# The first batch's biases added on GpSimd in SBUF, instead of by products with a row of ones

## The chip, the cores and the metric

One core of one Trainium2 chip runs the whole program. The metric is the device time of one launch in microseconds (us), median of several runs; less is better. TensorE does the matrix products (PE in the profile, its weight loads PEld), VectorE is DVE, ScalarE is ACT, GpSimd is POOL, and SyncE (SP) issues all of this kernel's DMAs, in order.

## The reference

For each of 8 batches of 3008 rows with 256 columns: a real Fourier transform along the rows, a complex linear layer on each frequency, a soft threshold at 0.01, the inverse transform, and then a feed-forward block on all 24064 rows.

```
X  = rfft(x, axis=1)
Yr = Xr @ w_r - Xi @ w_i + b_r
Yi = Xr @ w_i + Xi @ w_r + b_i
Y  = sign(Y) * max(|Y| - 0.01, 0)        # real and imaginary part apart
x2 = irfft(Y).reshape(24064, 256)
h  = x2 @ w_in                           # 256 -> 2048
out = (h - tanh(h)) @ w_out              # 2048 -> 256
```

## The kernel before

**Three products for the complex layer.** With the sum s = Xr + Xi there is one common product t1 = s @ w_r, and the two parts are Yr = t1 + Xi @ w3 + b_r and Yi = t1 + Xr @ w2 + b_i, where w3 = -(w_r + w_i) and w2 = w_i - w_r. The two products that belong to one part each stand side by side in one PSUM bank, `vv` (512 columns), and t1 has a bank of its own (256 columns, tag `o0`, a single buffer).

**Stages.** At the start the first batch's rows are transformed over one factor of the length (L291) and written to DRAM (`a`). Then comes the stage of the change: twelve units (`WholeSpectrum`, L516), which share out the frequencies of the first batch, go through the second transform (`dft`, L534), the linear layer (`cross`, L544; the last unit `cross_apart`, L559), the threshold and the first step of the inverse (`inverse`, L605), and write to DRAM (`z`). After the stage the second inverse step (L667) makes the first two chunks of rows, and the feed-forward block starts (`up`, L703, and `down`, L733). All later batches go through the same mathematics in pieces laid between the products of the feed-forward block, by other functions (`Spectrum`, L376); their biases were added by VectorE from a tile `bias` already (L447).

**The loop over units (L854 to L900), and the order of the work.** Each engine runs its instructions in the order in which the program emits them. One pass of the loop is called turn i here. Turn i emits, among others:

- `common` of unit i-2: ScalarE copies t1 out of PSUM into `tb`
- `dft` of unit i: TensorE's products, and ScalarE's copy `xf`
- on ScalarE, from turn 3 on, steps of a weight conversion (`ends` is two activations, `parts` a cast with a subtraction on GpSimd, L250)
- `shrink` of unit i-2: VectorE's `blend` adds tb and vv (L579), then ScalarE's `above` and `below` (L586, L590)
- `sum` of unit i on VectorE (L542), which `cross` of unit i needs one turn later
- `cross` of unit i-1 on TensorE; its t1 reuses the one bank, so it waits for the ScalarE copy of the unit before
- in even turns the inverse of units i-4 and i-3, with four ScalarE copies `zo`
- in turns 2, 3 and 4 one split of a linear weight in two parts (`split_lin`, L818): a ScalarE cast, and a subtraction, in turns 2 and 4 on GpSimd and in turn 3 on VectorE
- on VectorE the rest of the weight conversion (L221 to L245), and `join` of unit i-2 (L603), which the inverse needs

In the last turn `sum` comes ahead of `shrink`. After the loop units 10 and 11 are finished in a row of their own (L901 to L919).

**The weight conversion.** The feed-forward weights come as 64-bit floats and are turned into pairs of 32-bit words block by block, by the steps named above; the blocks' raw words (`w_raw`) are loaded by SP, the first at the end of turn 0.

**The biases before.** 33 partitions of SBUF get the two biases in one row (L165, called from L160). `combine_linear` (L168) makes from them a tile `brow` in which row 0 holds the rounded bias, row 32 what the rounding left, and all others zero, and a tile `ones`. In `cross` one product of `ones` with `brow` (L551; L567 twice in `cross_apart`) writes the biases into vv before the other products add to it.

**SP's order around the stage.** SP issues the stores of `a` (L309, L313) and the first units' loads (`at`, L388); the last four L313 stores are followed by turn 0's load of the first `w_raw` (L195), and then by turn 1's load `at` of unit 4, which needs those stores landed.

Of the kernel before, what the change touches and what calls it, by code (L numbers as in the profile page):

```python
# [92 lines left out]


@with_exitstack
def spectral_ffn(ctx, tc, x, w_r, w_i, w_in, w_out, x_fold, b_turned, f1, f1b, f1f, f2, f2f, i1, i1w, i2, out):
    nc = tc.nc
    P = 128
    w_in, w_out = w_in.bitcast(U32), w_out.bitcast(U32)
# [55 lines left out]
    def load_linear():  # L155
        wr = ffn.tile([P, 2, D], F32, name="wr_f", tag="g_h")
        wi = ffn.tile([P, 2, D], F32, name="wi_f", tag="g_l")
        nc.sync.dma_start(out=wr, in_=w_r.rearrange("(t p) e -> p t e", p=P))
        nc.sync.dma_start(out=wi, in_=w_i.rearrange("(t p) e -> p t e", p=P))
        rows = load_bias(work.tile([33, 2, D], F32, name="bias_rows", tag="tmp", bufs=4), 33)  # L160
        return wr, wi, rows

    def load_bias(dst, n):
        both = b_turned.rearrange("(o k) d -> o (k d)", o=1).to_broadcast([n, 2 * D])
        nc.sync.dma_start(out=dst.rearrange("p k d -> p (k d)"), in_=both)  # L165
        return dst

    def combine_linear(wr, wi, rows, zero):  # L168
        w2 = ffn.tile([P, 2, D], F32, name="w2_f", tag="g_h")
        w3 = ffn.tile([P, 2, D], F32, name="w3_f", tag="g_h")  # L170
        nc.vector.scalar_tensor_tensor(out=w3, in0=wr, scalar=-1.0, in1=wi, op0=ALU.mult, op1=ALU.subtract)
        nc.gpsimd.tensor_tensor(out=w2, in0=wi, in1=wr, op=ALU.subtract)
        ones = work.tile([P, P], F32R, name="ones", tag="s_l")
        nc.vector.tensor_scalar(out=ones, in0=zero[:, :P], scalar1=1.0, scalar2=None, op0=ALU.add)
        top = work.tile([33, 2 * D], F32R, name="bias_top", tag="tmp", bufs=4)
        flat = rows.rearrange("o r e -> o (r e)")
        nc.scalar.copy(out=top, in_=flat)
        brow = work.tile([P, 2 * D], F32R, name="brow", tag="ot", bufs=1)
        nc.vector.tensor_copy(out=brow, in_=zero)
        nc.vector.tensor_copy(out=brow[0:1], in_=top[0:1].bitcast(F32))  # L180
        nc.vector.tensor_tensor(out=brow[32:33], in0=flat[32:33], in1=top[32:33].bitcast(F32), op=ALU.subtract)
        return (wr, w2, w3), (ones, brow)

    win_h = const.tile([P, 2, FF], F32R, name="win_h")
    win_l = const.tile([P, 2, FF], F32R, name="win_l")
# [330 lines left out]
    class WholeSpectrum(Spectrum):  # L516
# [27 lines left out]
        def cross(self):  # L544
            if self.jp % 3 < 2:
                self.vv = ps_h.tile([P, 512], F32, name="ps_v", tag="h")
            else:
                self.vv = ps_o.tile([P, 512], F32, name="ps_v", tag="o1")
            ones, brow = bias_rows
            by_part = self.vv.rearrange("p (r i j) -> p r i j", r=2, j=2)  # L550
            nc.tensor.matmul(by_part, ones, brow.rearrange("p (r j i) -> p r i j", r=2, j=2), start=True, stop=False)  # L551
            self.t1 = ps_o.tile([P, 512], F32, name="ps_t1", tag="o0")[:, :D]
            for k, (dst, lhs) in enumerate((
                (self.vv[:, :D], self.xf[:, :, 1]), (self.vv[:, D:], self.xf[:, :, 0]), (self.t1, self.sf),
            )):
                for t in range(2):
                    nc.tensor.matmul(dst, lhs[:, t], whole_lin[2 - k][:, t, :], start=k == 2 and t == 0, stop=k > 0 and t == 1)

        def cross_apart(self):  # L559
            ones, brow = bias_rows  # L560
# [4 lines left out]
            for dst, lhs, w, b in ((self.t1, self.sf, 0, None), (low, self.xf[:, :, 1], 2, 0), (high, self.xf[:, :, 0], 1, D)):  # L565
                if b is not None:
                    nc.tensor.matmul(paired(dst, D), ones, in_turn(brow[:, b:b + D]), start=True, stop=False)  # L567
                for t in range(2):
                    nc.tensor.matmul(dst, lhs[:, t], whole_lin[w][:, t, :], start=b is None and t == 0, stop=t == 1)

        def common(self):
            self.tb = work.tile([P, D], F32, name="tb0", tag="xi")
            nc.scalar.copy(out=self.tb, in_=self.t1)

        def blend(self):
            self.y = self.temp("y", "g")
            if not hasattr(self, "sides"):
                both = self.vv.rearrange("p (r d) -> p r d", r=2)
                nc.vector.tensor_tensor(out=self.y, in0=self.tb.unsqueeze(1).to_broadcast([P, 2, D]), in1=both, op=ALU.add)  # L579
                return  # L580
            for r, side in enumerate(self.sides):
                nc.vector.tensor_tensor(out=self.y[:, r], in0=self.tb, in1=side, op=ALU.add)

        def above(self):
            self.up = self.temp("up", "th")
# [180 lines left out]
    with tc.manual_schedule(engines={E.PE, E.Activation, E.DVE, E.Pool, E.SP}):  # L766
# [18 lines left out]
        lin_in = load_linear()  # L785
# [68 lines left out]
        for i in range(NU):  # L854
            if i + 2 == NU:
                for c in range(2):
                    waves[c].tile()
                    waves[c].load_part(0, LATE - 8)
            if i + 1 == NU:
                for c in range(2):  # L860
                    waves[c].load_part(LATE - 8, LATE)
            if unit(i - 2):
                unit(i - 2).common()
            unit(i).dft()
            if i + 1 == NU:
                unit(i).sum()
            for op in on_act.get(i, ()):
                op()
            if unit(i - 2):
                unit(i - 2).shrink()  # L870
            if i + 1 < NU:
                unit(i).sum()
            if unit(i - 1):
                unit(i - 1).cross()
            if 0 < i < NU - 3:
                units[i + 3].load()
            if i in turns:
                load_turns(*units[turns[i]:turns[i] + 2])
            if i == NU - 3:
                for u in units[-4:]:  # L880
                    u.load_turn()
            if i > 2 and i % 2 == 0:
                pair = units[i - 4:i - 2]
                pair[1].inverse(banks=pair[0].inverse(), first=D)
                for u in pair:
                    u.put()
            if i < len(early):
                early[i].load()
            if i == 4:
# [94 lines left out]
        for g in range(-2, FIXED):  # L984
            c, f = steps[g + 2]
            ready[g + 2] = chunks[c].up(f, plan.get(g, ()))
            if g == -2:
                forward(6)
                forward(7)
                blocks[1].load()  # L990
                load_bias(bias, P)
# [163 lines left out]
```

## Time and profile before

| | us |
|---|---|
| median of three runs (2443.18 to 2443.49) | 2443.32 |
| the profiled execution | 2442.45 |
| its span, first to last instruction | 2440.7 |

| engine | busy us | share of the span | instructions |
|---|---|---|---|
| PE | 2429.0 | 100% | 19274 |
| DVE | 1779.9 | 73% | 3251 |
| ACT | 1348.6 | 55% | 2781 |
| POOL | 34.5 | 1% | 31 |

The shares are means over the whole program. The stage of the change lies between 25.7 and 85 us, so it has to be read by stretches of its own. A timeline row gives the start of an instruction, its duration, its engine and line, and in brackets how long the engine was idle before it and what ended that. The chain of waits gives start, length and what the end of the program hung on at that time. The granted TensorE clock is a share of full speed: 1.00 is 2.4 GHz, 0.50 is 1.2 GHz.

### The profile page before, as it was taken

To read this page: it belongs to the slowest core of one execution; us is meant where nothing else is said; L and a number is where in the kernel's file an instruction comes from. 1 tells how busy PE (TensorE), PEld (TensorE's weight loads), DVE (VectorE), ACT (ScalarE), POOL (GpSimd) and SP (SyncE) were. 2 spreads that over 40 slices of the span, in tenths; PEclk is the share of its full clock that TensorE was granted. 3 is DMA by queue.
4 is the path that set the end of the run, shared out by engine and by line. 5 is a ranking of instruction groups with operands and counts; after the bars stand their busy time and mean duration, and the time that the engine had idled before them with its cause. 6 is when DMAs were issued, how large, how long until landed. Compare 5 with 4: busy or idle time off the path is not lost.

```text
span 2440.7 us, 47556 instructions
## 1 busy us (share of the span) xinstructions
PE 2429.0 (100%) x19274; PEld 2139.4 (88%) x19274; DVE 1779.9 (73%) x3251; ACT 1348.6 (55%) x2781; POOL 34.5 (1%) x31
## 2 busy tenths in 40 slices
PE   9999999999999999999999999999999999999999
PEld 6798888888888898888888889888898999888888
DVE  5887887787777776777767777677776767755555
ACT  5665555555555555555555555555555555555554
POOL 2110000000000000000000000000000000000000
PEclk9999999999999999999999999999999999999999
DMA  8533226322533212332123331322211121111000
GB/s 262 183 100 113 84 67 152 92 74 78 145 87 105 79 53 66 98 98 69 61 71 101 82 94 53 81 82 80 63 61 46 59 58 43 52 34 26 21 9 17
DMA packets 135146, 195.31 MB, mean 80 GB/s; under 512 B 13521, under 2 KB 99631, under 8 KB 134928
## 3 DMA queue, kind: packets, MB, share of 16 engines
q1 hardware_dynamic: 134928, 192.29, 27.3%
q8 instruction: 151, 2.47, 0.4%
q14 instruction: 67, 0.55, 0.1%
HBM read 114.12 MB, written 78.12 MB: 79 GB/s over the span
## 4 chain that ended last, share of the span: by engine, by line
PE 93%; DVE 4%; ACT 1%; DMA 1%; issue 0%; SPq 0%; ACTq 0%; DVEq 0%
PE o L742 39%; PE h L709 38%; PE ps_v L423 4%; PE ps_i L667 3%; PE ps_t L423 2%; PE ps_f L507 2%; PE ps_f L343 1%; DVE g L723 1%; PE ps_i L479 1%; PE ps_i L480 1%; PE ps_i L478 1%; PE ps_f L291 1%; DVE gl L729 1%; DVE w_s L242 0%; DVE w_f L239 0%
## 5 line engine op out<-in xcount | busy, mean ns | idle before, releaser
L726 ACT CAST gh<-g 128x502 fp32r<-128x502 f32 (+2 forms) x768 | 469.1, 611 | 570.7 <-DVE g L723 561.1
L729 DVE TENSOR_TENSOR gl<-g,gh 128x502 fp32r<-128x502 f32 (+2 forms) x768 | 522.1, 680 | 332.0 <-ACT gh L726 322.0
L723 DVE TENSOR_TENSOR g<-h,th 128x502 f32<-128x502 f32 (+2 forms) x768 | 520.4, 678 | 219.7 <-ACT th L720 214.5
L720 ACT ACTIVATE th<-h 128x502 f32<-128x502 f32 (+2 forms) x768 | 454.1, 591 | 379.1 <-PE h L709 374.8
L742 PE MATMUL o<-gh,wout_l 128*128 128x502 f32 (+2 forms) x1536 | 587.6, 383 | 0.2 <-DVE ot L760 0.2
L742 PE MATMUL o<-gh,wout_h 128*128 128x502 f32 (+2 forms) x1536 | 576.9, 376 | 0.0
L742 PE MATMUL o<-gl,wout_h 128*128 128x502 f32 (+2 forms) x1536 | 576.5, 375 | 0.0
L709 PE MATMUL h<-yh,win_l 128*128 128x502 f32 (+2 forms) x1536 | 452.6, 376 | 1.1 <-DVE g L723 1.0
L709 PE MATMUL h<-yh,win_h 128*128 128x502 f32 (+2 forms) x1536 | 451.0, 375 | 0.0
L709 PE MATMUL h<-yl,win_h 128*128 128x502 f32 (+2 forms) x1536 | 450.7, 375 | 0.0
L742 PEld LDWEIGHTS o<-gh,wout_l 128*128 128x128 f32 x1536 | 290.4, 189 | 53.8 <-issue 11.7
L709 PEld LDWEIGHTS h<-yh,win_l 128*128 128x128 f32 x1536 | 289.3, 189 | 39.3 <-DVE g L723 4.1
L742 PEld LDWEIGHTS o<-gl,wout_h 128*128 128x128 f32 x1536 | 290.4, 189 | 35.5 <-DVE gl L729 0.8
L709 PEld LDWEIGHTS h<-yh,win_h 128*128 128x128 f32 x1536 | 291.0, 189 | 34.3 <-issue 0.2
L709 PEld LDWEIGHTS h<-yl,win_h 128*128 128x128 f32 x1536 | 291.1, 190 | 33.9
L742 PEld LDWEIGHTS o<-gh,wout_h 128*128 128x128 f32 x1536 | 291.0, 189 | 26.4
L465 DVE TENSOR_TENSOR y<-tb,ps_v 64x256 f32<-64x256 f32 x336 | 140.0, 417 | 3.4
L700 ACT CAST yh<-yt 128x470 fp32r<-128x470 f32 (+38 forms) x200 | 89.4, 480 | 23.4 <-PE h L709 21.6
L701 DVE TENSOR_TENSOR yl<-yt,yh 128x470 fp32r<-128x470 f32 (+38 forms) x200 | 81.9, 428 | 16.0 <-ACT yh L700 15.1
L411 DVE TENSOR_TENSOR xl<-ps_f,xh 128x256 fp32r<-128x256 f32 x168 | 63.6, 419 | 27.5 <-ACT xi L409 26.0
L667 PEld LDWEIGHTS ps_i<-i,zin 48*64 48x64 f32 x4096 | 67.1, 138 | 9.5 <-issue 5.4
L667 PE MATMUL ps_i<-i,zin 48*64 48x47 f32 x4096 | 72.6, 235 | 1.6 <-DMA zin<-z 1.6
(116 smaller groups left out, 2110.3 us busy)
## 6 DMA issues: line engine op xcount, KB each, us to landing
xt<-in_x_fold SPq DMA_DIRECT2D x52, 512.0 KB
at<-a SPq DMA_DIRECT2D x96, 256.0 KB
z<-zo SPq DMA_DIRECT2D x92, 256.0 KB
zin<-z SPq DMA_DIRECT2D x92, 240.0 KB
a<-st SPq DMA_DIRECT2D x216, 96.0 KB
out<-ot SPq DMA_DIRECT2D x29, 502.0 KB
turn_l<-turns SPq DMA_DIRECT2D x72, 128.0 KB
turn_h<-turns SPq DMA_DIRECT2D x72, 128.0 KB
```

The costliest lines, as they stand in the source:

```text
L411: nc.vector.tensor_tensor(out=xl[:, s], in0=whole[s], in1=xh[:, s].bitcast(F32), op=ALU.subtract)
L423: nc.tensor.matmul(paired(dst, D), lhs[:, t], in_turn(rhs[:, t, :]), start=n == 0, stop=n == 5)
L465: nc.vector.tensor_tensor(out=self.y[ri * 64:(ri + 1) * 64, jj, :], in0=self.tb[rows, ri, :], in1=self.side(ri)[rows], op=ALU.add,)
L667: nc.tensor.matmul(pv[h][64 * c:64 * c + 64, t, 47 * k:47 * k + 47], self.zt[rows, k, at:at + 64], i2t[rows, :47], start=True, stop=True,)
L700: nc.scalar.copy(out=yh, in_=y)
L701: nc.vector.tensor_tensor(out=yl, in0=y, in1=yh.bitcast(F32), op=ALU.subtract)
L709: nc.tensor.matmul(paired(h, n), lhs[:, t, f * P:(f + 1) * P], moving(rhs[:, t], n), start=k == 0, stop=k == 5,)
L720: nc.scalar.activation(out=th[:, :n], in_=h[:, :n], func=AF.Tanh)
L723: nc.vector.tensor_tensor(out=g[:, :n], in0=h[:, :n], in1=th[:, :n], op=ALU.subtract)
L726: nc.scalar.copy(out=gh[:, :n], in_=g[:, :n])
L729: nc.vector.tensor_tensor(out=gl[:, :n], in0=g[:, :n], in1=gh[:, :n].bitcast(F32), op=ALU.subtract)
L742: nc.tensor.matmul(paired(self.o[t], n), lhs[:, f, t * P:(t + 1) * P], in_turn(rhs[:, :n]), start=f == 0 and k == 0, stop=f == NF - 1 and ...
```

## The change

The products with the row of ones go, with the tiles `brow` and `ones` and the load of 33 rows. The two biases are loaded into `bias` on all 128 partitions (256 KB) right after the last stores of `a`, ahead of the first `w_raw`. `common` still copies t1 by ScalarE, and then GpSimd adds t1's copy, taken twice, and the two biases into a tile `tb` of 512 columns; `blend` adds that to vv. For units 10 and 11 a VectorE instruction adds t1 from PSUM and the biases (`common_at_once`). `sum` comes ahead of `shrink` in every turn. Later, the load that filled `bias` for the other batches overwrites it with the biases in their other order.

```diff
@@ load_linear, load_bias, combine_linear
-        rows = load_bias(work.tile([33, 2, D], F32, name="bias_rows", tag="tmp", bufs=4), 33)
-        return wr, wi, rows
-    def load_bias(dst, n):
-        both = b_turned.rearrange("(o k) d -> o (k d)", o=1).to_broadcast([n, 2 * D])
+    def load_bias(dst, biases):
+        both = biases.rearrange("(o k) d -> o (k d)", o=1).to_broadcast([P, 2 * D])
         nc.sync.dma_start(out=dst.rearrange("p k d -> p (k d)"), in_=both)
...
-        ones = work.tile([P, P], F32R, name="ones", tag="s_l")
-        nc.vector.tensor_scalar(out=ones, in0=zero[:, :P], scalar1=1.0, scalar2=None, op0=ALU.add)
...
-        nc.scalar.copy(out=top, in_=flat)
-        brow = work.tile([P, 2 * D], F32R, name="brow", tag="ot", bufs=1)
-        nc.vector.tensor_copy(out=brow, in_=zero)
-        nc.vector.tensor_copy(out=brow[0:1], in_=top[0:1].bitcast(F32))
-        nc.vector.tensor_tensor(out=brow[32:33], in0=flat[32:33], in1=top[32:33].bitcast(F32), op=ALU.subtract)
@@ cross (cross_apart likewise)
-            nc.tensor.matmul(by_part, ones, brow.rearrange("p (r j i) -> p r i j", r=2, j=2), start=True, stop=False)
...
-                    nc.tensor.matmul(dst, lhs[:, t], whole_lin[2 - k][:, t, :], start=k == 2 and t == 0, stop=k > 0 and t == 1)
+                    nc.tensor.matmul(dst, lhs[:, t], whole_lin[2 - k][:, t, :], start=t == 0, stop=t == 1)
@@ common, blend
-            self.tb = work.tile([P, D], F32, name="tb0", tag="xi")
-            nc.scalar.copy(out=self.tb, in_=self.t1)
+            tb = work.tile([P, D], F32, name="tb0", tag="xi")
+            nc.scalar.copy(out=tb, in_=self.t1)
+            self.tb = work.tile([P, 2, D], F32, name="tb", tag="ot", bufs=1)
+            nc.gpsimd.tensor_tensor(out=self.tb, in0=tb.unsqueeze(1).to_broadcast([P, 2, D]), in1=bias, op=ALU.add)
+        def common_at_once(self):
+            self.tb = work.tile([P, 2, D], F32, name="tb", tag="ot", bufs=1)
+            nc.vector.tensor_tensor(out=self.tb, in0=self.t1.unsqueeze(1).to_broadcast([P, 2, D]), in1=bias, op=ALU.add)
...
-                nc.vector.tensor_tensor(out=self.y, in0=self.tb.unsqueeze(1).to_broadcast([P, 2, D]), in1=both, op=ALU.add)
+                nc.vector.tensor_tensor(out=self.y, in0=self.tb, in1=both, op=ALU.add)
@@ before the loop, after the last stores of a
-        whole_lin, bias_rows = combine_linear(*lin_in, zero)
+        load_bias(bias, b_plain)
+        whole_lin = combine_linear(*lin_in)
@@ the loop over units
             unit(i).dft()
-            if i + 1 == NU:
-                unit(i).sum()
+            unit(i).sum()
             for op in on_act.get(i, ()):
                 op()
             if unit(i - 2):
                 unit(i - 2).shrink()
-            if i + 1 < NU:
-                unit(i).sum()
@@ after the loop
-        u10.common()
+        u10.common_at_once()
         u11.cross_apart()
         u10.blend()
         u10.threshold()
-        u11.common()
+        u11.common_at_once()
```

## Rows read from the trace of the kernel before

**Rows 1.** Windows: stretch, length, busy us of PE PEld DVE ACT POOL, PEclk, DMA.

```profile
25.70:47.40 21.70, 21.15 (x125) 18.13 (x125) 10.27 (x20) 13.58 (x25) 1.80 (x2) 1.00 0.80 277
47.40:63.90 16.50, 16.49 (x100) 13.65 (x101) 14.23 (x24) 14.62 (x29) 6.00 (x4) 1.00 0.85 281
63.90:77.50 13.60, 13.38 (x79) 11.29 (x79) 12.71 (x22) 11.40 (x25) 3.91 (x3) 1.00 0.75 216
...
85.00:92.00 7.00, 5.45 (x13) 2.08 (x13) 5.38 (x10) 4.26 (x8) 0.10 (x1) 1.00 0.29 88
92.00:97.00 5.00, 4.98 (x161) 4.91 (x162) 1.86 (x5) 2.51 (x6) 2.40 (x2) 0.51 0.83 249
...
107.00:163.00 56.00, 55.01 (x277) 51.63 (x275) 55.05 (x89) 38.31 (x70) 10.36 (x8) 1.00 0.41 122
163.00:2440.70 2277.70, 2272.33 (x18376) 2011.48 (x18376) 1659.32 (x3045) 1245.94 (x2588) 0.00 (x0) 1.00 0.25 72
```

**Rows 2.** Chain of waits, 20 to 60 us: start, length, what.

```profile
30.15 5.28 DMA w_raw<-in_moe_w_in
...
37.13 0.61 DVE y L579
...
46.07 1.01 ACT w_h L142
...
47.41 1.13 PE ps_t L557 x4
```

**Rows 3.** Chain of waits, 60 to 86 us.

```profile
75.85 0.34 DVE w_s L221
...
83.88 1.16 PE ps_i L612 x8
```

**Rows 4.** Timeline of PE, two neighbours in turn 6.

```profile
49.19 0.46 PE L551 MATMUL ps_v<-brow,ones 128*128 128x512 f32 x1
49.49 1.89 PE L557 MATMUL ps_v<-w_f,xf 128*128 128x256 f32 x8
```

**Rows 5.** Timeline of SP, issue of the first block's load.

```profile
30.15 1.34 SPq L195 DMA_DIRECT2D w_raw<-in_moe_w_in  x1
```

**Rows 6.** Waits of SP's queue, 0 to 110 us: total, times, longest.

```profile
SPq L388 <- DMA a<-st: 2.3, 1, 2.3
```

**Rows 7.** Timeline of ACT in turns 2, 3 and 5.

```profile
31.93 0.72 ACT L586 ACTIVATE up<-y,column 128x512 f32<-128x512 f32 x1
...
33.17 1.10 ACT L142 CAST w_h<-wr_f 128x512 fp32r<-128x512 f32 x1
34.26 0.37 ACT L573 COPY tb<-ps_t 128x256 f32<-128x256 f32 x1
...
49.65 0.71 ACT L586 ACTIVATE up<-y,column 128x512 f32<-128x512 f32 x1
```

**Rows 8.** Timeline of POOL, 15 to 110 us.

```profile
18.02 1.26 POOL L172 TENSOR_TENSOR w_f<-wi_f,wr_f 128x512 f32<-128x512 f32 x1 [9.18 <-DMA wi_f<-in_w_i]
34.35 1.56 POOL L143 TENSOR_TENSOR w_l<-wr_f,w_h 128x512 fp32r<-128x512 f32 x1 [15.06 <-ACT w_h L142]
...
67.81 1.33 POOL L250 TENSOR_TENSOR wout_l<-w_f,wout_h 128x512 fp32r<-128x512 f32 x1 [4.78 <-ACT wout_h L249]
```

**Rows 9.** Timeline of DVE, five instructions of the stage and after it.

```profile
30.96 0.69 DVE L579 TENSOR_TENSOR y<-tb,ps_v 128x512 f32<-128x512 f32 x1 [2.17 <-ACT tb L573]
...
41.73 0.69 DVE L242 SCALAR_TENSOR_TENSOR w_s<-w_raw,w_s 128x512 uint32<-128x512 uint32 x1
...
67.92 1.77 DVE L242 SCALAR_TENSOR_TENSOR w_s<-w_raw,w_s 128x512 uint32<-128x512 uint32 x1
...
83.09 0.69 DVE L595 SCALAR_TENSOR_TENSOR mn<-y,mn 128x512 f32<-128x512 f32 x1
...
136.04 1.28 DVE L221 TENSOR_SCALAR w_s<-w_raw 128x512 uint32<-128x512 uint32 x1
```

**Rows 10.** Tile bias: the later batches' adds, ns min/median/max, first and last.

```profile
L447 DVE TENSOR_TENSOR tb<-ps_t,bias x84: 678/682/692, 238.1 to 2108.3; 128x512 f32<-128x512 f32 x84
```

More of the change, by code (lines that the diff above doesn't have):

```diff
@@ L95, in spectral_ffn @@
 @with_exitstack
-def spectral_ffn(ctx, tc, x, w_r, w_i, w_in, w_out, x_fold, b_turned, f1, f1b, f1f, f2, f2f, i1, i1w, i2, out):
+def spectral_ffn(ctx, tc, x, w_r, w_i, w_in, w_out, x_fold, b_plain, b_turned, f1, f1b, f1f, f2, f2f, i1, i1w, i2, out):
     nc = tc.nc
@@ L159, in load_linear, with combine_linear @@
         nc.sync.dma_start(out=wi, in_=w_i.rearrange("(t p) e -> p t e", p=P))
-        rows = load_bias(work.tile([33, 2, D], F32, name="bias_rows", tag="tmp", bufs=4), 33)
-        return wr, wi, rows
-    def load_bias(dst, n):
-        both = b_turned.rearrange("(o k) d -> o (k d)", o=1).to_broadcast([n, 2 * D])
+        return wr, wi
+    def load_bias(dst, biases):
+        both = biases.rearrange("(o k) d -> o (k d)", o=1).to_broadcast([P, 2 * D])
         nc.sync.dma_start(out=dst.rearrange("p k d -> p (k d)"), in_=both)
-        return dst
-    def combine_linear(wr, wi, rows, zero):
+    def combine_linear(wr, wi):
         w2 = ffn.tile([P, 2, D], F32, name="w2_f", tag="g_h")
@@ L172, in combine_linear @@
         nc.gpsimd.tensor_tensor(out=w2, in0=wi, in1=wr, op=ALU.subtract)
-        ones = work.tile([P, P], F32R, name="ones", tag="s_l")
-        nc.vector.tensor_scalar(out=ones, in0=zero[:, :P], scalar1=1.0, scalar2=None, op0=ALU.add)
-        top = work.tile([33, 2 * D], F32R, name="bias_top", tag="tmp", bufs=4)
-        flat = rows.rearrange("o r e -> o (r e)")
-        nc.scalar.copy(out=top, in_=flat)
-        brow = work.tile([P, 2 * D], F32R, name="brow", tag="ot", bufs=1)
-        nc.vector.tensor_copy(out=brow, in_=zero)
-        nc.vector.tensor_copy(out=brow[0:1], in_=top[0:1].bitcast(F32))
-        nc.vector.tensor_tensor(out=brow[32:33], in0=flat[32:33], in1=top[32:33].bitcast(F32), op=ALU.subtract)
-        return (wr, w2, w3), (ones, brow)
+        return wr, w2, w3
     win_h = const.tile([P, 2, FF], F32R, name="win_h")
@@ L548, in cross @@
                 self.vv = ps_o.tile([P, 512], F32, name="ps_v", tag="o1")
-            ones, brow = bias_rows
-            by_part = self.vv.rearrange("p (r i j) -> p r i j", r=2, j=2)
-            nc.tensor.matmul(by_part, ones, brow.rearrange("p (r j i) -> p r i j", r=2, j=2), start=True, stop=False)
             self.t1 = ps_o.tile([P, 512], F32, name="ps_t1", tag="o0")[:, :D]
@@ L556, in cross @@
                 for t in range(2):
-                    nc.tensor.matmul(dst, lhs[:, t], whole_lin[2 - k][:, t, :], start=k == 2 and t == 0, stop=k > 0 and t == 1)
+                    nc.tensor.matmul(dst, lhs[:, t], whole_lin[2 - k][:, t, :], start=t == 0, stop=t == 1)
         def cross_apart(self):
-            ones, brow = bias_rows
             self.t1 = ps_f.tile([P, 512], F32, name="ps_t1", tag="f")[:, :D]
@@ L564, in cross_apart @@
             self.sides = low, high
-            for dst, lhs, w, b in ((self.t1, self.sf, 0, None), (low, self.xf[:, :, 1], 2, 0), (high, self.xf[:, :, 0], 1, D)):
-                if b is not None:
-                    nc.tensor.matmul(paired(dst, D), ones, in_turn(brow[:, b:b + D]), start=True, stop=False)
+            for dst, lhs, w in ((self.t1, self.sf, 0), (low, self.xf[:, :, 1], 2), (high, self.xf[:, :, 0], 1)):
                 for t in range(2):
-                    nc.tensor.matmul(dst, lhs[:, t], whole_lin[w][:, t, :], start=b is None and t == 0, stop=t == 1)
+                    nc.tensor.matmul(dst, lhs[:, t], whole_lin[w][:, t, :], start=t == 0, stop=t == 1)
         def common(self):
-            self.tb = work.tile([P, D], F32, name="tb0", tag="xi")
-            nc.scalar.copy(out=self.tb, in_=self.t1)
+            tb = work.tile([P, D], F32, name="tb0", tag="xi")
[5 more added lines that the diff above has]
+            nc.vector.tensor_tensor(out=self.tb, in0=self.t1.unsqueeze(1).to_broadcast([P, 2, D]), in1=bias, op=ALU.add)
         def blend(self):
@@ L578, in blend @@
                 both = self.vv.rearrange("p (r d) -> p r d", r=2)
-                nc.vector.tensor_tensor(out=self.y, in0=self.tb.unsqueeze(1).to_broadcast([P, 2, D]), in1=both, op=ALU.add)
+                nc.vector.tensor_tensor(out=self.y, in0=self.tb, in1=both, op=ALU.add)
                 return
             for r, side in enumerate(self.sides):
-                nc.vector.tensor_tensor(out=self.y[:, r], in0=self.tb, in1=side, op=ALU.add)
+                nc.vector.tensor_tensor(out=self.y[:, r], in0=self.tb[:, r], in1=side, op=ALU.add)
         def above(self):
@@ L990, in spectral_ffn @@
                 blocks[1].load()
-                load_bias(bias, P)
+                load_bias(bias, b_turned)
                 for k in (2, 3):
@@ L1138 @@
     given["x_fold"] = given["x_fold"].reshape(B - 1, 128, 4, 2, 2, 2 * D)
-    given["b_turned"] = np.ascontiguousarray(np.stack([given.pop("b_r"), given.pop("b_i")])[:, back], np.float32)
+    given["b_plain"] = np.stack([given.pop("b_r"), given.pop("b_i")]).astype(np.float32)
+    given["b_turned"] = np.ascontiguousarray(given["b_plain"][:, back])
     given |= dict(zip(("f1", "f1b", "f1f", "f2", "f2f", "i1", "i1w", "i2"), dft_constants()))
```

## The prediction

> **What bounds the kernel now.** I read the busy times by stretches first, then the chain of waits through the stage of the change, then the timelines of the four engines and of SP in it. The stretches [rows 1] show that the share of the whole span says nothing here. From 163 us to the end PE is busy 2272.33 of 2277.70 us, and from 107 to 163 us DVE is busy 55.05 of 56.00. Neither has room, so whatever the stage before loses or wins arrives at the end unreduced. The stage itself has three parts. Up to 47.4 us the chain [rows 2] runs through waits: the first block of feed-forward weights lands 5.28 us after its issue at 30.15, then DVE's blend of unit 1 (37.13) and ACT's in-order queue follow, until a cast at 46.07 and the copy behind it release t1's single bank at 47.41. From there to 63.9 PE is busy 16.49 of 16.50 us: PE ends last. From 63.9 to 77.5 DVE is busy 12.71 of 13.60, the chain goes through DVE's weight conversion, and the stage ends with the inverse at 83.88 [rows 3].
>
> **What goes.** Ten products with `ones` in the loop and one before it, eleven in all, and two in `cross_apart`. Start to start such a product takes 0.30 us (49.19 to 49.49, [rows 4]). So PE is freed of 13 x 0.30 = 3.9 us, but only those in the stretch that PE bounds can move the end: the three of turns 6 to 8, 0.9 us. The work that made `brow` lies before 25.7 us, when DVE and ACT wait for the first units, and gives nothing.
>
> **The bias load, and the first add.** Before, no step of unit 0 needed the biases by DMA so late. Now add(0) on POOL waits for 256 KB whose issue stands where the first w_raw load stood, 30.15. That load's issue took 1.34 us [rows 5], and then SP waited 2.3 us for the stores of a [rows 6]: 30.15 + 1.34 + 2.3 = 33.8, when the stores ahead of it had landed; w_raw itself was there at 35.43. The bias load takes its place in the same queue of transfers, between these two, so it lands between 33.8 and 35.4. It has half of w_raw's bytes, so I take 34.2, nearer to the stores. Outer ends: 32.5, if its packets pass the last store's, and 35.5. Then add(0). No add of this form stands in the trace; the nearest is the plain 512-column one, 1.26 us, the other end the one with strided operands, 1.56 [rows 8]. I take 1.27 with the step to the next engine: 35.5. Blend(0), before at 30.96 [rows 9], takes 0.69, so ACT's `above` of unit 0 starts at 36.2 instead of 31.93 [rows 7]: 4.3 us late. ACT is in order, so the cast of the first weight split (33.17) and the copy of t1 of unit 1 (34.26), both behind it [rows 7], are 4.3 late too. TensorE is not: it goes on until unit 2's t1 wants the bank that this copy frees.
>
> **Turns 3 to 5.** POOL is in order as well. Its first split (34.35, 1.56) waits for the cast, which now ends at 33.17 + 1.10 + 4.3 = 38.6; split and add(1) take 1.5 + 1.27, so blend(1) comes at 41.4 instead of 37.13 in the chain: still 4.3 late. From there the chain to 47.41 is one unbroken row of ACT, DVE and PE, and shifts whole. One new piece enters it: add(2) becomes ready while DVE splits the second weight, gets its turn behind that, and DVE's next instruction waits for it: 1.27, with blend(2)'s wait for the shifted `sum` 0.3 more. So t1 and its copy in turn 5 are 5.9 late. Then add(3) stands behind POOL's third split, which starts when the cast of 46.07 ends, at 47.1 + 5.9 = 53.0; with 1.5 + 1.27 blend(3) starts at 55.8 and `above` at 56.5, where it was at 49.65 [rows 7]. **After turn 5: 6.9 us late.** ACT's conversion steps ahead of `above` hid the rest of POOL's 2.8.
>
> **The port that DVE and POOL share.** This prices the other turns. At 67.81 POOL subtracts for 1.33 us; DVE's L242, which starts beside it at 67.92 and reads two SBUF tiles, takes 1.77 where it takes 0.69 with POOL idle [rows 8, 9]: 1.08 lost. A one-input instruction, L221, shows the same: 1.28 [rows 9] against 0.34 [rows 3]. By the Trainium skill (SBUF — State Buffer, section "Who interferes with whom") DVE and GpSimd share a port pair as an exclusive lock, and an instruction with two SBUF inputs, or in a two-port mode, fully blocks against GpSimd; the trace agrees with its 1.08. By that rule a blend, with one input in PSUM, goes free, so the rule bears on what runs around it.
>
> Each turn now has one more POOL instruction of 1.27. Of what DVE does in a turn only `sum` (0.33 from start to start, moved ahead for that) and blend go beside it, and blend waits for it. So an add costs DVE up to 1.27 - 0.33 = 0.94. In 47.4 to 63.9 DVE has 16.50 - 14.23 = 2.27 us of idle time, 0.65 in each of 3.5 turns, which hides that much: 0.3 a turn in turns 6 to 8. In 63.9 to 77.5 it has 0.89 us in nearly three turns; I count nothing of it, so turns 9, 10 and 11 pay 0.94 each. Together 0.9 + 2.8 = **3.7 us**. Bounds: 0 (every add under a wait) and six times 1.56, 9.4. The 0.9 us that PE gives back are not subtracted, since ACT and DVE are behind PE by then; if PE still ended last they would be.
>
> **The end.** `common_at_once` puts two adds from PSUM into DVE's queue; the same instruction of the later batches takes 0.682 [rows 10], about 0.60 from start to start, so 1.2 us, where ACT's copies lay beside other work. DVE's last step for unit 11 ended at 83.09 + 0.69 = 83.78, just ahead of the inverse at 83.88: 0.1 hides. **1.1 us.** Bounds 0.5 and 1.4. The stage's waits on DMA (z out and in, 85 to 92) follow its last copies and shift with them.
>
> **Sum.** 6.9 + 3.7 + 1.1 = 11.7 us. The profiled execution took 2442.45 (span 2440.7), so the changed kernel's would take 2454.2; the median of the runs shown is 0.87 above that execution, so 2455.0.
>
> **Rivals.**
>
> *The adds hide, only the start is late.* POOL is idle for most of the stage, and if its adds fall where DVE waits, the 3.7 go and turn 5's 2.6 beyond the start with them. 4.3 + 1.1 = 5.4, so 2448.7. Against it: DVE has hardly a gap from 63.9 on. Chance 0.14.
>
> *The clock falls inside the stage.* PE was granted 0.51, the 1.2 GHz level, from 92 on, after a stretch in which it was busy 5.45 of 7.00 us [rows 1]. With t1's bank waiting in turns 3 to 5, PE will idle for 2 to 3 us at a time between 36 and 54. Its 16.49 us over three and a half turns are 4.7 a turn, 4.4 without the product; at half the clock up to 8.8, against some 6 that DVE then needs: 2 to 3 us more in one or two turns, say 4 us, so 2459. Against it: with that much idle time PE has room. By the Trainium skill (TensorE: Matmul & The Clock Gate, Part 1) the throttled state is the default and activity releases it; the 0.51 agrees. Chance 0.12.
>
> *Not slower: the matrix engine decides throughout.* If the biases have landed when t1 of unit 0 is copied (just before blend(0) at 30.96), add(0) delays blend(0) by 1.3 us only, ACT catches up under its casts, and PE is last all the way. Then what counts is 0.9 us (three products) to 3.9 us (all): 2442.4 to 2439.4, within 0.2% of now. It decides at the landing: any later than about 32 us, and `above` of unit 0 holds ACT. For it: PE is busy 21.15 of 21.70 us even in the first part. Against it: the stores ahead are in flight until 33.8. Chance 0.08.
>
> **How the numbers follow.** The forecast has 0.66, with 2450 to 2460 as its own range. A measurement of this kernel can tell about 0.2%, 4.9 us, from no change. The bounds give 4.3 - 1.7 + 2.6 + 0 + 0.5 = 5.7 at the low end, 2449, and with a landing at 35.5 (+1.3), adds of 1.56 in turns 2 to 5 (+1.2), 9.4 and 1.4 at the high end 20.2, 2463.5. The range 2449 to 2462 leaves out the third rival, about half of the first and the far high end. Slower 0.90: the forecast, the second rival and most of the first. Same 0.08, faster 0.02.
>
> **What would show it.** POOL's add(0) starts near 34.2, released by the DMA of the bias; blend(0) near 35.5; t1 of unit 4 near 53; the blends of turns 9 and 10 some 8 to 10 us later than before; L239 to L245 and L603 stretched to 1.3 to 1.9 in most turns; the last inverse near 95.6. From 107 us (then 119) on nothing but a shift. The forecast is wrong if add(0) starts before 32, or if the delay at the last inverse isn't that at the end, or if DVE's instructions keep their lengths.

## The result, and the profile after

The changed kernel takes 2457.26 us (median of 4 runs, 2455.40 to 2458.59) against 2443.25 us (4 runs on the same chip): ratio 1.0056, 95% interval 1.0044 to 1.0069, 14.0 us slower. The forecast was 2455.0. The profiled execution of after, the longest of its four, took 2458.59 (span 2456.8), 16.1 us more than that of before. The last inverse starts at 99.19 where it started at 83.88 [rows 3], 15.3 us late, so all but 0.8 us of the loss is made in the stage.

Windows of after; lengths, busy us of PE, PEld, DVE, ACT, POOL, then granted clock, DMA share, GB/s:

```profile
25.70:47.40 21.70, 17.44 (x86) 15.16 (x85) 5.74 (x11) 9.63 (x16) 5.01 (x4) 0.84 0.83 276
47.40:63.90 16.50, 13.37 (x82) 9.79 (x81) 12.55 (x20) 10.48 (x20) 6.31 (x5) 1.00 0.49 151
...
107.00:120.00 13.00, 12.92 (x191) 10.99 (x191) 7.07 (x15) 7.38 (x16) 2.50 (x2) 0.74 0.72 207
120.00:177.00 57.00, 56.96 (x287) 53.58 (x285) 55.26 (x89) 40.20 (x73) 10.09 (x8) 1.00 0.42 126
177.00:2456.80 2279.80, 2272.74 (x18377) 2009.52 (x18376) 1660.60 (x3047) 1246.74 (x2588) 0.26 (x1) 1.00 0.25 72
```

Against [rows 1]: PE, busy 21.15 of the first 21.70 us before, now has 4.3 us of idle time there, and from 47.4 to 63.9 it has 3.1 where it had 0.01. The last two windows are as before, only shifted.

The chain of waits through the stage in after (start, length, what), the counterpart of [rows 2, 3]:

```profile
29.65 6.01 DMA bias<-in_b_plain
...
35.80 1.26 POOL tb L558
...
40.22 1.53 POOL w_l L143
41.76 1.23 POOL tb L558
...
43.02 0.70 DVE y L568
...
45.07 1.00 ACT w_h L142
...
46.10 1.08 DVE w_l L143
47.18 1.63 DVE w_f L228
48.81 0.60 DVE w_s L231
49.42 0.60 DVE mn L592
50.02 0.33 DVE sf L531
50.35 0.60 DVE y L568
...
54.72 1.15 PE ps_t L543 x4
...
99.19 1.16 PE ps_i L601 x8
```

It begins in the biases' load, 6.01 us, goes over POOL's add to unit 0, over a split and the next add on POOL, and from 46.10 over DVE, where one instruction of 0.69 (L228) takes 1.71 (its row is below; 1.63 in the chain). Behind 54.72 the view names a load of w_raw (56.35 to 61.87), but DVE has no gap from 57.30 to 65.7, so the stage did not wait for that load. ACT in after, the step `above` of units 0, 3 and 9 (31.93 and 49.65 for the first two before, [rows 7]):

```profile
37.81 0.72 ACT L575 ACTIVATE up<-y,column 128x512 f32<-128x512 f32 x1 [6.00 <-DVE y L568]
...
58.02 0.72 ACT L575 ACTIVATE up<-y,column 128x512 f32<-128x512 f32 x1 [0.97 <-DVE y L568]
...
91.87 0.72 ACT L575 ACTIVATE up<-y,column 128x512 f32<-128x512 f32 x1 [3.72 <-DVE y L568]
```

So the delay is 5.9 us at the first unit and 8.4 in turn 5. At unit 9 it is 13.8, since there `above` stood at 78.09 before, and at the last inverse 15.3. POOL and then DVE in after (counterparts of [rows 8, 9]):

```profile
35.80 1.26 POOL L558 TENSOR_TENSOR tb<-tb,bias 128x512 f32<-128x512 f32 x1 [16.45 <-DMA bias<-in_b_plain]
...
46.41 1.86 POOL L558 TENSOR_TENSOR tb<-tb,bias 128x512 f32<-128x512 f32 x1 [3.43 <-ACT tb L556]
54.47 1.56 POOL L143 TENSOR_TENSOR w_l<-w_f,w_h 128x512 fp32r<-128x512 f32 x1 [6.20 <-ACT w_h L142]
55.99 1.27 POOL L558 TENSOR_TENSOR tb<-tb,bias 128x512 f32<-128x512 f32 x1
...
78.24 1.63 POOL L239 TENSOR_TENSOR wout_l<-w_f,wout_h 128x512 fp32r<-128x512 f32 x1 [2.44 <-ACT wout_h L238]
79.84 1.71 POOL L558 TENSOR_TENSOR tb<-tb,bias 128x512 f32<-128x512 f32 x1
```

```profile
37.09 0.69 DVE L568 TENSOR_TENSOR y<-tb,ps_v 128x512 f32<-128x512 f32 x1 [4.82 <-POOL tb L558]
...
47.10 1.71 DVE L228 SCALAR_TENSOR_TENSOR w_f<-w_raw,w_m 128x512 f32<-128x512 uint32 x1
...
57.30 0.69 DVE L568 TENSOR_TENSOR y<-tb,ps_v 128x512 f32<-128x512 f32 x1 [1.68 <-POOL tb L558]
...
78.66 1.75 DVE L231 SCALAR_TENSOR_TENSOR w_s<-w_raw,w_s 128x512 uint32<-128x512 uint32 x1
80.45 1.64 DVE L234 SCALAR_TENSOR_TENSOR w_f<-w_f,w_s 128x512 f32<-128x512 f32 x1
...
93.85 0.68 DVE L562 TENSOR_TENSOR tb<-ps_t,bias 128x512 f32<-128x512 f32 x1
...
96.36 0.69 DVE L562 TENSOR_TENSOR tb<-ps_t,bias 128x512 f32<-128x512 f32 x1
```

Two things are to be seen. Blends wait for POOL (4.82, 1.68). And POOL's `parts` and add, one behind the other from 78.24 to 81.55, stretch two DVE instructions in a row by 1.0 us each (78.66, 80.45), and are stretched themselves, from 1.27 to 1.63 and 1.71.

### The profile page after: what moved, and what is told of

The parts are those of the page before. It is cut to its first block, busy times and chain, and to the rows that moved or that the text cites. A ratio compares the mean times of both kernels' runs of the same rounds, so it can differ in the third digit from the quotient of the medians.

```text
span 2456.8 us, 47547 instructions
## 1 busy us (share of the span) xinstructions
PE 2432.3 (99%) x19261; PEld 2137.3 (87%) x19261; DVE 1786.4 (73%) x3249; ACT 1348.1 (55%) x2778; POOL 48.1 (2%) x41
## 4 chain that ended last, share of the span: by engine, by line
PE 91%; DVE 5%; DMA 1%; ACT 1%; issue 1%; SPq 0%; POOL 0%; ACTq 0%; DVEq 0%; POOLq 0%
PE o L731 38%; PE h L698 38%; PE ps_v L412 4%; PE ps_i L656 3%; PE ps_t L412 2%; PE ps_f L496 2%; PE ps_f L332 1%; DVE g L712 1%; PE ps_i L469 1%; PE ps_i L468 1%; PE ps_i L467 1%; DVE gl L718 1%; PE ps_f L280 1%; DMA xt<-in_x_fold 0%; DVE w_s L231 0%
## 5 line engine op out<-in xcount | busy, mean ns | idle before, releaser
L731 PEld LDWEIGHTS o<-gh,wout_l 128*128 128x128 f32 x1536 | 290.2, 189 | 54.1 <-issue 11.7
```

What stands on the lines that cost most here:

```text
L731: nc.tensor.matmul(paired(self.o[t], n), lhs[:, f, t * P:(t + 1) * P], in_turn(rhs[:, :n]), start=f == 0 and k == 0, stop=f == NF - 1 and ...
```

## Experiments

Single runs of one kernel lie 1 to 7 us apart, so I also measure the **stage** in each profile: from the start of PE's first dft matmul to the start of the last inverse. One profile each: before, e5 and e11 run the same instructions up to `above` of unit 0 (e5 one product more) and reach it 6.2, 6.5 and 7.2 us after that first matmul, so a stage is good to about 1 us. "Rest" is from the last inverse to the end of the span. Ratios are to before on the same chip (medians 2442.3 to 2443.3). The first batch's biases are left out in e2, e3, e7, e8, e9 and e12.

| kernel | stage | rest | median us (low to high) | ratio to before, 95% |
|---|---|---|---|---|
| before | 58.2 | 2356.8 | 2443.25 | |
| after | 73.9 | 2357.6 | 2457.26 | 1.0056 [1.0044, 1.0069] |
| e1 load early | 70.1 | 2357.1 | 2454.86 (2452.01 to 2458.63) | 1.0051 [1.0036, 1.0066] |
| e2 no biases | 59.5 | 2357.3 | 2441.81 (2440.26 to 2445.67) | 0.9996 [0.9987, 1.0006] |
| e3 adds beside | 69.2 | 2357.6 | 2453.84 (2453.35 to 2454.52) | 1.0046 [1.0031, 1.0061] |
| e4 all on VectorE | 72.2 | 2354.1 | 2452.63 (2451.64 to 2454.21) | 1.0042 [1.0027, 1.0057] |
| e5 products twice | 59.1 | 2360.3 | 2446.48 (2444.79 to 2448.11) | 1.0012 [1.0002, 1.0021] |
| e6 early and VectorE | 67.1 | 2353.6 | 2448.03 (2446.60 to 2453.69) | 1.0024 [1.0015, 1.0033] |
| e7 memset aside | 60.3 | 2353.4 | 2440.97 (2440.34 to 2442.64) | 0.9993 [0.9983, 1.0002] |
| e8 add aside, 384 | 62.9 | 2353.8 | 2443.54 (2442.81 to 2444.16) | 1.0001 [0.9992, 1.0011] |
| e9 early and beside | 67.9 | 2355.0 | 2450.50 (2448.55 to 2453.52) | 1.0033 [1.0021, 1.0045] |
| e10 sums as before | 73.2 | 2357.2 | 2456.83 (2456.26 to 2458.71) | 1.0059 [1.0044, 1.0074] |
| e11 parts on VectorE | 59.5 | 2357.1 | 2442.32 (2440.74 to 2445.93) | 0.9999 [0.9990, 1.0009] |
| e12 add aside, 512 | 64.8 | 2357.9 | 2447.21 (2445.51 to 2450.40) | 1.0019 [1.0010, 1.0029] |

**e1: the biases' load moved ahead, right behind that of the linear weights.**

```diff
+        bias = const.tile([P, 2, D], F32, name="bias")
         lin_in = load_linear()
+        load_bias(bias, b_plain)
...
-        bias = const.tile([P, 2, D], F32, name="bias")
...
-        load_bias(bias, b_plain)
         whole_lin = combine_linear(*lin_in)
```

> The changed kernel, but the 256 KB of biases are loaded right after the linear weights, some 20 us earlier. Theory (three costs in a row: the late landing, GpSimd's adds in the chain and on the shared port, two adds at the end): add(0) no longer waits for a DMA, ACT's first step on unit 0 comes near 33.3 instead of 37.8 and the first weight block lands 1.5 us earlier again; 3 to 5 us of the 14 go, 2452 to 2454. Rival A (the landing is covered by ACT's casts and by the weight block that DVE waits for anyway): within 1 us of 2457. Rival B (the landing is the whole loss): back to 2443 to 2445.

Measured: POOL's first add at 31.86, `above` of unit 0 at 33.97 instead of 37.81, but the last inverse only 3.8 us earlier from the stage's start, and the median only 2.4: 2454.86 is just above the theory's 2452 to 2454, and in neither rival's bounds. Of 15.7 us in the stage nearly 12 remain with the biases there in time. The late landing is not the larger part, and what is left is more than I had put down for the port.

**e2: no adds, no load, no products; sums ahead of blend as in after.**

```diff
-            nc.gpsimd.tensor_tensor(out=self.tb, in0=tb.unsqueeze(1).to_broadcast([P, 2, D]), in1=bias, op=ALU.add)
+            self.tb = tb
...
-        load_bias(bias, b_plain)
...
-        u10.common_at_once()
+        u10.common()
```

> The changed kernel without any bias in the first batch: no load, no adds, the sums of frequencies first, blend reads ScalarE's copy as before. It leaves the biases of the first batch out. Theory (only the products of the stretch that PE bounds are worth something): 2441 to 2443, at most 2 us faster than before. Rival C (PE bounds the whole stage, so all 13 products at 0.30 us are won): 2439 to 2440. Rival D (the earlier place of the sums costs by itself): slower than 2444.

Measured as the theory had it: with everything of the change but the adds and their load, the kernel is as fast as before. The loss is in these two: the adds (on GpSimd, and two on VectorE) and the load.

**e3: e2 with the load in place and the GpSimd adds written to a tile that nobody reads (`common_alone`, for units 10 and 11, is the copy without an add).**

```diff
             self.tb = tb
+            aside = work.tile([P, 2, D], F32, name="aside", tag="ot", bufs=1)
+            nc.gpsimd.tensor_tensor(out=aside, in0=tb.unsqueeze(1).to_broadcast([P, 2, D]), in1=bias, op=ALU.add)
...
-        u10.common()
+        u10.common_alone()
```

> As the run without biases, but the bias load stands where the change put it and GpSimd makes its ten adds into a tile that nobody reads; it leaves the biases out of the result. So the adds take the port and GpSimd's queue, but are in no chain. Theory: the port alone costs DVE about 0.9 us in each of the last three turns and 0.3 to 0.5 in the others, and the first weight block is 1.5 us late behind the load: 2447 to 2450. Rival E (the port costs nothing, only the waits for the adds do): 2442 to 2444.5. Rival F (the port is the whole loss): 2454 to 2457.

My expectation failed: 2453.84 lies between its 2447 to 2450 and the 2454 of rival F. No blend waits for an add, and still the stage is 9.7 us longer than e2's. That an add runs is enough. Two causes were mixed here, since the late load also makes the first adds and POOL's split come in a row; e9 takes them apart.

**e9: e3 with the load moved as in e1.**

> The GpSimd adds go to a tile that nobody reads (the biases are left out of the first batch), and the biases are loaded early, so that the adds neither delay a blend nor bunch behind a load. What is left against the kernel without biases (stage 59.54 us, 2441.8 us) is what the adds cost the other work by running beside it. Theory (that by itself is most of the loss): the stage from the first dft to the last inverse takes 65 to 68.5 us and the kernel 2448 to 2452 us. Rival P (the adds cost only when they bunch behind the late load, as in the run with the adds beside and the load in place; otherwise my 0.94 us an add on half of them at most): 61 to 64 us, 2443 to 2447 us. If the stage reaches the 70.1 us of the early load with adds in the chain, the wait of blend for the add costs nothing at all.

Measured: stage 67.9, 2450.5 us, as the theory had it. DVE's groups in the stage, 25 to 100 us (count, busy us, mean ns of one, idle time before), first of e2 and then of e9:

```profile
L231 DVE SCALAR_TENSOR_TENSOR w_s<-w_raw,w_s 128x512 uint32<-128x512 uint32 x8 | 8.7, 1088 | 0.0
...
L234 DVE SCALAR_TENSOR_TENSOR w_f<-w_f,w_s 128x512 f32<-128x512 f32 x8 | 6.2, 781 | 0.1
L228 DVE SCALAR_TENSOR_TENSOR w_f<-w_raw,w_m 128x512 f32<-128x512 uint32 x8 | 5.5, 693 | 2.8 <-ACT w_s L221 2.2 <-issue 0.3
...
L210 DVE TENSOR_SCALAR w_s<-w_raw 128x512 uint32<-128x512 uint32 x8 | 3.4, 420 | 2.0 <-DMA w_raw<-in_moe_w_in 2.0
L225 DVE TENSOR_SCALAR w_m<-w_raw 128x512 uint32<-128x512 uint32 x8 | 3.4, 420 | 0.0
```

```profile
L231 DVE SCALAR_TENSOR_TENSOR w_s<-w_raw,w_s 128x512 uint32<-128x512 uint32 x8 | 8.7, 1086 | 0.0
...
L228 DVE SCALAR_TENSOR_TENSOR w_f<-w_raw,w_m 128x512 f32<-128x512 uint32 x8 | 7.3, 908 | 2.5 <-ACT w_s L221 2.2
L234 DVE SCALAR_TENSOR_TENSOR w_f<-w_f,w_s 128x512 f32<-128x512 f32 x7 | 6.8, 972 | 0.1
L210 DVE TENSOR_SCALAR w_s<-w_raw 128x512 uint32<-128x512 uint32 x8 | 6.1, 767 | 3.2 <-DMA w_raw<-in_moe_w_in 3.2
L225 DVE TENSOR_SCALAR w_m<-w_raw 128x512 uint32<-128x512 uint32 x8 | 5.6, 704 | 0.0
```

L228, L234, L210 and L225 got longer by 1.7, 1.3, 2.8 and 2.3 us (difference of the means times the count), 8.1 in all; the join got 0.3 shorter. L231 was held by POOL's `parts` already. The stage grew by 8.4, but not all of that is VectorE's time. From the first dft matmul to `above` of unit 9 e9 takes 7.6 us more than e2 (61.3 and 53.7). Behind that e9's clock was granted 0.54 from 87.3 to 90.5, and PE's products for unit 11, in e2 and then in e9, show it:

```profile
81.22 1.89 PE L552 MATMUL ps_v<-w_f,xf 128*128 128x256 f32 x8
```

```profile
87.29 3.33 PE L552 MATMUL ps_v<-w_f,xf 128*128 128x256 f32 x8
```

In e9 PE then runs without a gap into the last inverse (93.44), 0.9 us after VectorE's last step for unit 11 had ended (92.58), so some 0.8 us of the 8.4 are the clock's. The port term alone is about **7.6 us**.

**e7, e8 and e12: e2 with a GpSimd instruction aside, behind each blend but the last.** A memset of 8 columns of the copy of t1 keeps it behind the blend. Then comes one of the last three lines: a memset of 128 x 1024 (0.95 us; writes only), an add of two 384-column operands (1.0 us), or an add of two 512-column ones, as long as the change's (`flat` is a flat view of the linear weights, one in e8 and a list of two in e12; its line is not shown):

```diff
                 nc.vector.tensor_tensor(out=self.y, in0=self.tb.unsqueeze(1).to_broadcast([P, 2, D]), in1=both, op=ALU.add)
+                nc.gpsimd.memset(self.tb[:, :8], 0.0)
+                aside = work.tile([P, 2, 512], F32, name="aside", tag="ot", bufs=1)
+                nc.gpsimd.memset(aside, 0.0)                  # e7
+                nc.gpsimd.tensor_tensor(out=aside[:, 0, :384], in0=flat[:, :384], in1=flat[:, 128:], op=ALU.add)   # e8
+                nc.gpsimd.tensor_tensor(out=aside.rearrange("p r e -> p (r e)")[:, :512], in0=flat[0], in1=flat[1], op=ALU.add)   # e12
```

> The run without biases (they are left out), and after each blend of the loop GpSimd writes zeros into a tile nobody reads, 1024 columns, some 0.95 us: GpSimd busy beside VectorE's two-input steps, but reading no SBUF. Theory (what two-input steps meet is GpSimd's read port): within 1.5 us of the run without biases, 2441 to 2443. Rival I (any GpSimd instruction beside them holds them): 2447 to 2451.

> As the run with zeros, but GpSimd adds two SBUF tiles, 384 columns, some 0.95 us, at the same place. The biases are left out. Theory (the shared port, 0.7 to 0.9 us for each of ten adds, seven or more of them on the path): 2447 to 2451. Rival E (the port costs nothing, the loss of the run with adds beside came from its late load): 2441 to 2444.

> As the run with an aside add behind each blend (384 columns, 1.0 us, stage 62.86 us, 2443.5 us), but 512 columns wide, so the add has the length of the change's (about 1.27 us) and only its place differs: right behind blend, where the change and the early adds beside have it at the copy of t1. Theory (the place decides: behind blend the add falls on above's wait and on instructions that DVE has room for): stage 63 to 65 us, 2443 to 2446 us. Rival L (the length decides: an add of 1.27 us there holds as many instructions as at the copy of t1, where the stage took 67.89 us): stage 66 to 69 us, 2447 to 2450.5 us.

e7 came as expected. e8 did not: 2443.54 is below the theory's 2447 to 2451 and inside the bounds of rival E, by which the port costs nothing. That isn't so either, as e8's runs all lie above e7's and its stage is 2.5 us longer; but it is far from a whole add a turn. e12's stage (64.8) is the theory's, its time (2447.2) the rival's. The time can't decide here: e12's profile has a stretch at the low clock behind the stage (granted 0.63 from 98 to 107) that e8's hasn't, and three of its ten runs, with a mean clock of 1.00, took 2445.5 to 2445.9. By the stages both have a part: 1.0 to 1.27 us of length is worth 1.9 us, and the place, behind blend (eleven adds, no load) rather than at the copy of t1 (e9: ten adds, an early load), some 3. POOL and DVE side by side, in e7 and then in e12:

```profile
64.76 0.94 POOL L570 MEMSET aside<- 128x1024 f32 x1
...
65.36 0.69 DVE L234 SCALAR_TENSOR_TENSOR w_f<-w_f,w_s 128x512 f32<-128x512 f32 x1
...
82.25 0.95 POOL L570 MEMSET aside<- 128x1024 f32 x1
...
82.19 1.29 DVE L585 TENSOR_SCALAR mn<-y 128x512 f32<-128x512 f32 x1
```

```profile
56.61 1.56 POOL L571 TENSOR_TENSOR aside<-wr_f,w_f 128x512 f32<-128x512 f32 x1
...
56.95 1.76 DVE L228 SCALAR_TENSOR_TENSOR w_f<-w_raw,w_m 128x512 f32<-128x512 uint32 x1
```

The memset leaves an instruction with two operands in SBUF at its 0.69; the add holds one for 1.07. By the Trainium skill (SBUF — State Buffer, section "Who interferes with whom") such an instruction contends with a GpSimd instruction that reads SBUF and not with one that only writes it; the trace agrees. The memset is not free for every instruction, though: L585, with one operand, took 1.29 beside the memset at 82.25 and 0.43 without one (84.91). Few such instructions fell beside a memset (L210 at 45.91 took 0.87, L225 at 60.67 0.74), so e7 lost little.

**e4 and e6: all twelve adds on VectorE from PSUM, with the load in place (e4) and early (e6).**

```diff
             if unit(i - 2):
-                unit(i - 2).common()
+                unit(i - 2).common_at_once()
```

> The changed kernel with the bias add of every unit done by VectorE from PSUM, as it does for the last two units: no ScalarE copy, no add on GpSimd, the load where the change put it. Theory: ten adds of 0.60 us on DVE where it is full from turn 9 on, and the late landing of about 5 us at the start stay; the port's cost and GpSimd's queue go: 2450 to 2453. Rival G (what counts is DVE's time, and 0.60 of its own is as dear as an add beside it): 2455 to 2458.

> The changed kernel with the early load and all bias adds on VectorE. Theory (landing and port both gone, twelve adds of 0.60 us on DVE left, of which those of the last turns and the two at the end are on the path): 4 to 7 us slower than before, 2447 to 2450. Rival H (without landing and port DVE has room for the adds): 2442 to 2444. Rival G (DVE's time is all that counts, as dear as the port): 2453 or more.

Both medians fell within the theory's bounds, with some luck, as the windows below will show. DVE's group of adds in e4 and then in e6:

```profile
L562 DVE TENSOR_TENSOR tb<-ps_t,bias 128x512 f32<-128x512 f32 x12 | 8.2, 684 | 7.3 <-DMA bias<-in_b_plain 7.3
```

```profile
L562 DVE TENSOR_TENSOR tb<-ps_t,bias 128x512 f32<-128x512 f32 x12 | 8.2, 683 | 1.6 <-PE ps_t L543 1.6
```

With the load early, e6's stage is 7.5 us longer than e2's; twelve adds at 0.60 from start to start are 7.2. GpSimd's ten adds in the same position, with the last two on VectorE (e1), cost 10.6. Not having them on VectorE saved nothing: VectorE paid for them anyway, and more. e4 pays 5.1 us for the landing.

The two profiles gained some 3 us outside the stage, which no theory had. Windows of e6 behind it:

```profile
98.00:107.00 9.00, 8.13 (x177) 5.44 (x177) 7.33 (x14) 5.94 (x12) 2.51 (x2) 1.00 0.69 210
107.00:120.00 13.00, 13.00 (x66) 11.98 (x65) 11.26 (x21) 10.15 (x19) 0.00 (x0) 1.00 0.77 240
```

The clock stays at 2.4 GHz here, where after was granted 0.74 from 107 to 120, that is a loss of 13 x 0.26 = 3.4 us at 1.2 GHz with PE busy throughout. Before has the like from 92 on [rows 1]. The "rest" is 2356.8 to 2357.9 in the profiles with this stretch (before, after, e1, e2, e3, e10, e11, e12) and 2353.4 to 2355.0 in those without it (e4, e6, e7, e8, e9). So medians of neighbours must be read with 3 us of care: if the runs behind their medians lack it like their profiles, e4 would be near 2456 with it, in rival G's range, and e6 near 2451, above the theory's. The profiles of before and after both have it, so it is no part of their difference.

**e5: before, with each bias product issued twice (`cross_apart` likewise).**

```diff
-            nc.tensor.matmul(by_part, ones, brow.rearrange("p (r j i) -> p r i j", r=2, j=2), start=True, stop=False)
+            for last in (True, False):
+                nc.tensor.matmul(by_part, ones, brow.rearrange("p (r j i) -> p r i j", r=2, j=2), start=True, stop=last)
...
```

> The kernel before with every bias product made twice (the second overwrites the first), 13 products more. Theory (only the three of the stretch that PE bounds move the end): 0.9 us slower than before, up to 1.5. Rival C (PE bounds the stage throughout): 3.9 us slower, 2446.8.

The stage grew by 0.9 us, what the theory had, but no more than the 1 us to which a stage is good. The rest grew by 3.5, and only half of that is a lower clock: from 92 to 107 e5 was granted 0.66 and before 0.77, a difference of 15 x 0.11 = 1.7 us. The other 1.8 are not traced. The median, 2446.48, is nearer to rival C's 2446.8, and the ratio's interval (0.5 to 5.1 us) holds both theories, so e5 alone decides nothing. That the products cost little in the stage is e2's evidence.

**e10: after, with the sums behind shrink as before.**

```diff
-            unit(i).sum()
+            if i + 1 == NU:
+                unit(i).sum()
...
+            if i + 1 < NU:
+                unit(i).sum()
```

> The changed kernel with the sums put back behind shrink, as before the change; all else as changed. Theory (the order of the sums is a term of about 1 us either way; the adds are the loss): 2456 to 2460 us, stage 73 to 77 us, because now the sum waits on VectorE's queue behind a blend that waits for an add, and cross starts later. Rival O (putting the sum ahead of blend is itself what costs, as it delays blend): 2450 to 2454 us.

Within the theory's bounds (the stage, 73.2, too), and equal to after (2456.83 and 2457.26). The order of the sums makes no difference that can be told.

**e11: before, with the subtraction of `parts` of the first six blocks on VectorE instead of GpSimd.**

```diff
+        def low_part(self):
+            hi, lo = places(*self.at)
+            nc.vector.tensor_tensor(out=lo, in0=self.w, in1=hi.bitcast(F32), op=ALU.subtract)
...
-            5: [b1.fraction, b1.scale, b2.exponent, b2.mantissa],
+            5: [b0.low_part, b1.fraction, b1.scale, b2.exponent, b2.mantissa],
```

> The kernel before, with the subtraction of parts (GpSimd, two operands in SBUF) in the stage moved to VectorE for the first six blocks, behind the join of the turn before. Theory (a GpSimd instruction that reads SBUF costs VectorE's two-operand instructions beside it about its own length less the overlap, so that VectorE doing the same work itself in 0.6 to 0.7 us costs no more): 2440.5 to 2443.5 us, the instructions of VectorE over 1 us in the stage fall from 5 to 2 or less. Rival W (VectorE has no room for 6 x 0.69 = 4.1 us more): 2444.5 to 2447 us.

Measured 2442.32, no different from before, and the instructions of VectorE over 1 us in the stage fell from 5 to 2, as expected. A group of DVE's in before and two in e11:

```profile
L242 DVE SCALAR_TENSOR_TENSOR w_s<-w_raw,w_s 128x512 uint32<-128x512 uint32 x8 | 8.7, 1088 | 0.0
```

```profile
L242 DVE SCALAR_TENSOR_TENSOR w_s<-w_raw,w_s 128x512 uint32<-128x512 uint32 x8 | 5.5, 685 | 0.0
...
L257 DVE TENSOR_TENSOR win_l<-w_f,win_h 128x512 fp32r<-128x512 f32 x4 | 2.9, 733 | 0.6 <-ACT win_h L253 0.6
```

L242 averaged 1088 ns in before and 685 here. VectorE does six subtractions more, 4.3 us, and the kernel takes them for nothing: L242 and the join got shorter by 4.0 us together when GpSimd's were gone. No version with the biases in it beat before.

## Why the prediction was right, and where its terms were off

The direction, the size and the place were right. Its terms 4.3, 2.6, 3.7 and 1.1 came out as 5.9, 2.5, 5.4 and 1.5, by the delay of `above` of units 0, 3 and 9 and of the last inverse. Two of them, the landing and the port, were too small, and no error made up for another: the stage lost 15.3 us where 11.7 were forecast, and the medians 14.0.

- **The late landing.** Taken at 34.2, with 35.5 as the outer end; it came at 35.66, 6.01 us after an issue at 29.65. 256 KB behind the stores took longer than the 5.28 of w_raw with its 512 KB [rows 2]. The choice of the near end for its half of the bytes was the error; the step from landing to `above` held (2.0 predicted, 2.1 seen). As a part of the whole its worth is 3.8 us (after against e1): the delay at unit 0 falls by 5 us from the stage's start and the stage by 3.8.
- **Turns 3 to 5.** 2.6 predicted, 2.5 seen. add(3) stands behind the third split as said (54.47, 55.99), and blend(3) waits 1.68 for it. The step before it held as well: DVE's next instruction behind the second split, L228, is held by add(2), 1.63 in the chain instead of 0.6, so 1.0 where 1.27 was predicted; and blend(2) comes behind the `sum` (0.33), as said.
- **The port in turns 6 to 11: the mis-sized term.** 3.7 predicted, 5.4 seen. I let 2.27 us of DVE's idle time hide part of three adds and counted 0.94 each for three more. The step that was wrong is that only `sum` and blend go beside an add. In e9, where no blend waits for an add, `above` falls behind e7 by 2.1 us up to unit 3 and 5.6 more by unit 9: the whole of turns 6 to 11 comes back with adds that nobody reads. And the port does not begin at turn 6: over the stage it is about 7.6 us, with a part of the turns 3 to 5 in it. The idle time hid little, since an add that starts at the copy of t1 finds DVE still at conversion steps ahead of its blend (in after L225 at 59.90 and L210 at 74.59 and 87.41, at 1.49 to 1.50 instead of 0.42), and where `parts` precedes it, DVE is held twice in a row (78.66 and 80.45). A blend goes free, as said: at 57.30 it took its 0.69 beside `parts` (57.21, 1.28). Of the signs named, the blends of turns 9 and 10 came 11.5 and 12.0 us later, not 8 to 10, and the join (L592 in after) kept its 0.69, while L210 and L225 (L221 and L236 in before), which the list left out, were stretched.
- **The end.** Two adds at 0.68, 0.60 from start to start; 1.5 against 1.1.
- **Behind the stage** a shift, as said: 15.3 at the last inverse, 16.1 at the end.
- **The rivals.** *The adds hide* is out by e9. *The matrix engine decides throughout* falls with the landing at 35.66 and with PE's idle time. *The clock falls inside the stage* came true as an event and not as a cost: 0.84 in the first window, but from 35.80 to 54.4 the chain passes no PE instruction. At the end the view's chain follows PE, but PE's products before the last inverse had ended at 98.3, and DVE, continuous from 93.24 to 99.1, ends last.

Going from before to after step by step, the stage is 58.2, then 59.5 (products gone, sums first, +1.3, hardly more than the scatter), 67.9 (adds run beside and the load comes early, +8.4, some 0.8 of it the clock), 70.1 (blends wait for them and two adds go to VectorE, +2.2), 73.9 (load late, +3.8). What the early load costs by itself was not run alone; up to `above` of unit 0 e9 is not behind e2 (7.3 and 7.9 us). The medians, 2441.8, 2450.5, 2454.9 and 2457.3, tell the same order, with the clock behind the stage mixed in. How the 7.6 divides by turn is not settled to better than 1 us, and why the place behind blend is cheaper by some 3 was seen (e9 and e12) and not traced to single instructions.

## What to carry to other kernels

Work moved from a full engine to GpSimd is not off the path while VectorE is the engine that ends last: price each GpSimd instruction that reads SBUF at the time it holds those of VectorE's instructions beside it whose operands all lie in SBUF (here the ones with two and the conversion steps with one), over all turns and without credit for idle time that lies elsewhere in the turn. Compare it with VectorE doing the work itself (here 0.60 us an add against about 1). And a constant that a first step needs has to be issued ahead of the traffic it would queue behind; price its landing from the slowest neighbour in the queue, not from its bytes.

## What the runs showed that I had not expected

- A GpSimd memset of 0.95 us behind each blend costs next to nothing (e7, stage +0.8 over e2), an add of 1.0 us costs 2.5 in eleven places, one of 1.27 us 4.5 there and 7.6 in ten places at the copy of t1 (e8, e12, e9, against e7). But the memset, too, holds an instruction with one operand (L585 in e7, 1.29 instead of 0.43).
- VectorE's instructions with one operand (L210, L225) are held as the two-operand ones are: from 0.42 to a mean of 0.70 to 0.77 in e9. The prediction had one case of it [rows 9], which it set against the 0.34 of the chain, a length from start to start; a row of it alone is 0.42. It makes 5.1 of the 8.1 us.
- GpSimd pays too: its adds in after take 1.44 us on the mean, up to 1.86, against 1.26 undisturbed.
- Some 3 us of the kernel's time hang on whether the clock falls right behind the stage, whichever way the biases are added.
